# The input product of a fused RWKV-6 and GELU-MLP kernel: seven products of halves for tiles 2 to 7, and attention in finer, planned slots

## The chip, the cores and the metric

The kernel runs on one core of a Trainium2 chip. The metric is device time in microseconds; lower is better. The core has TensorE (matrix products, written to PSUM), VectorE, ScalarE and GpSimd (elementwise work), and queues that issue DMA transfers; SyncE and ScalarE issue the ones that matter here. Each engine takes its instructions in the order in which the program gives them, and waits where an operand isn't ready or a buffer isn't free.

## The reference

Two blocks follow each other. The first is RWKV-6 attention over 4 batches, 8 heads, 768 steps and 48 channels: a state per head decays by `w` at each step and takes up `k` times `v`. Its output, with the heads side by side, is the input of an MLP with an exact GELU, 384 to 2048 to 384, over 3072 tokens.

```python
for t in range(S):
    kt, vt, rt, wt = (k[:, :, t], v[:, :, t], r[:, :, t], w[:, :, t])
    cur = np.einsum('bhd,bhe->bhde', u[None] * kt, vt)
    y[:, :, t] = np.einsum('bhd,bhde->bhe', rt, state + cur)
    state = wt[:, :, :, None] * state + np.einsum('bhd,bhe->bhde', kt, vt)
...
h = x @ w_in
g = 0.5 * h * (1.0 + erf(h * inv_sqrt2))
return (g @ w_out).astype(np.float32)
```

## The kernel before

The 3072 tokens are cut into eight tiles of 384, two for each batch. For each tile there are two programs, both Python generators. `attention(x, unit)` (L318) issues the attention of tile x and leaves the output, transposed, in `xT`. `mlp(x)` (L782) turns `xT` into output rows. A loop at L1076 runs eight stages: in stage x it walks through `mlp(x - 1)` and, at the steps listed in `place`, lets `attention(x)` go on by one slot, that is up to its next `yield`; `place_next` does the same for the first slots of `attention(x + 1)`, and `times` for the pieces of the next tile's load. The order of the instructions on every engine follows from these lists alone. Tile 0 runs ahead of the loop with its own slots.

**Attention of tiles 2 to 7.** Time within a chunk of 64 steps is treated by quarters at two levels, `QUARTERS = (4, 16)`. First VectorE multiplies r, u and k (L356), makes running products of w (`tot`, L375), products for distances 1 to 3 within four steps (`apart`, L350) and their sums with a transposing reduction (L343), and folds w into r and k (L379). ScalarE (`plain`, L502) and VectorE (`lay_out`, L507 and L508) then lay out r for a level in `kx`. A burst of 96 small matmul records on 64x64 tiles of the array (L529, at the first level with L522 ahead of it) makes the blocks of a level in three pairs of PSUM banks, and VectorE copies them under a mask into `a_sb` (L560, L567). r and k are updated for the next level (L536, L542, L545). After the second level k is transposed in blocks (L481), moved by DMA (L476) and by ScalarE (L591), and three more bursts follow: k times v (L607) with the chain of states on VectorE (L622), blocks times v (L648), and r times states (L689). ScalarE copies the result to `xT` (L712); one quarter of the heads goes through `ysb` (L715) and six DMAs (L719).

**The MLP.** w_in (three chunks of 128 rows) and w_out stay in SBUF. For tiles 0 to 6 h is computed plainly: for each of 16 blocks of 128 columns three matmuls of 384 columns into one of two PSUM banks (L886), and GELU on ScalarE (L889, L891). The output product is done plainly for tile 0 (L1023), and for the others as seven products of halves, 192 columns wide (L900), with sums of g and of w_out made by VectorE; the last 128 rows of two tiles are combined likewise.

Only in the last tile is h itself made from seven products of halves (`h_halves`, L813, matmuls at L840), over the first two of the three chunks and both halves of tokens and columns; four products remain for the third chunk. Here VectorE adds the intermediate sums (L852 to L866), six PSUM banks are used, and attention is over. `h_sums` (L746) makes sums of w_in and differences of `xT` for it in the stage before. The third block of 128 rows of the last tile is a plain product (L929).

PSUM has eight banks: two, with the tag `mm`, serve h and the output products, and three pairs (`pd`, L91) serve attention.

Of the kernel before, what the change touches and what calls it, by code (L numbers as in the profile page):

```python
# [20 lines left out]
C = 64  # L21
# [15 lines left out]
HALFWAY = 2  # L37

# [6 lines left out]
def kernel(  # L45
# [45 lines left out]
    pd = pairs_of_banks.enter_context(tc.tile_pool(name="pd", bufs=3, space=PSUM))  # L91
# [29 lines left out]
    def load_v(x, dma):  # L121
        loaded[x][1] = io.tile([128, v.shape[2]], F32, name="v_in")
        dma.dma_start(out=loaded[x][1], in_=v[x])
# [10 lines left out]
    def load(x, dma):  # L134
# [4 lines left out]
        for i in range(3):  # L139
            if i == 1:  # L140
                load_v(x, dma)
                yield
            t = bufs[x % 2 if i == 0 else 1]
            for j in range(3):
                a = i * ALL + j * ALL // 3
                dma.dma_start(out=t[:, a:a + ALL // 3], in_=rkw[x, :, a:a + ALL // 3])
                yield

# [39 lines left out]
    def keep_warm(n, elsewhere=False):  # L188
        if elsewhere:
            t = pd.tile([128, 2, BANK], F32, name="warm", tag="d")[:, 0]  # L190
# [66 lines left out]
    def make_quarter_masks():  # L257
        make_fine()
        for (h, a), m_q in m_qs.items():
            nc.vector.tensor_tensor(out=quarter[h][a], in0=s_qs[h][:, 0:m_q.shape[1]], in1=m_q, op=ALU.is_equal)  # L260

# [3 lines left out]
    tot_sb = const.tile([128, NP * T], F32, name="tot_sb")  # L265

# [3 lines left out]
    def conversion():  # L270
# [5 lines left out]

        prepare(i + HALFWAY)
        if wide:
# [20 lines left out]
    def finish(dst, raw, f, e):  # L299
# [9 lines left out]
        nc.vector.tensor_scalar(out=f, in0=f, scalar1=3, scalar2=None, op0=ALU.logical_shift_left)  # L309
        nc.vector.scalar_tensor_tensor(out=e, in0=hi, scalar=0x80000000, in1=e,  # L310
# [7 lines left out]
    def attention(x, unit):  # L318
# [34 lines left out]
        if x >= 2:  # L353
            for q in range(qs):
# [3 lines left out]
                                               op0=ALU.mult, op1=ALU.mult)  # L358
            transposed_sums(0, 0, FINE)
# [11 lines left out]
        for h in LEVELS:  # L371
# [4 lines left out]
            at_tot += nb  # L376
        if x >= 2:
            def times(z, by):
                nc.vector.tensor_mul(z, z, by)  # L379

            places_of = [apart(1, 3)]
            times(k4[:, :, 0:2], w4[:, :, 1:3])
            places_of.append(apart(2, 2))
            times(k4[:, :, 0:1], w4[:, :, 2:3])
            places_of.append(apart(3, 1))
            yield
            for e, place in enumerate(places_of, 1):
                transposed_sums(place, e, FINE - e)

            w_01 = tot[2].rearrange("p (m two) -> p m two", two=2)[:, :, 0:1]  # L390
            times(k4[:, :, 0:3], w4[:, :, 3:4].to_broadcast([128, n_m, 3]))
            times(r4[:, :, 3:4], w4[:, :, 2:3])
# [6 lines left out]
        def products(bs, right, width):  # L399
            d = pd.tile([128, 2, BANK], F32, name="d", tag="d")  # L400
# [20 lines left out]
        def halves():  # L421

            for h in LEVELS:
# [9 lines left out]
                if h == 1:  # L433
                    yield
                    diag = diagonal()

# [13 lines left out]
                else:  # L450
                    nc.vector.tensor_mul(rk, rk, tt)  # L451
                ah = at.rearrange("p g n (m two j) -> p g n m two j", two=2, j=h)[:, :, :, :, 1, :]
# [16 lines left out]
        kt_q = w.rearrange("p (g n d) -> p g n d", g=2, d=G)  # L469
# [15 lines left out]
        def quarters():  # L485
# [26 lines left out]
            yield  # L512
            for h in QUARTERS:
                m, r4, t4, s0, s1, s2 = views(h)
                banks = [pd.tile([128, 2, BANK], F32, name="d", tag="d") for _ in range(0, np_ * NI, 4)]
                if h == FINE:

                    n_b = np_ * NI
                    fine_ps = [banks[-1][:, g, 6 * C:6 * C + FINE * n_b] for g in range(2)]
                    for a in range(FINE):  # L520
                        for g in range(2):
                            nc.tensor.matmul(fine_ps[g][:, a * n_b:], lhsT=places[half[g], a], rhs=fine_sb[half[g], 0:FINE - a, a],  # L522
                                             start=(a == 0), stop=True, skip_group_check=True)
                ds = []
                for n, d in zip(range(0, np_ * NI, 4), banks):
                    for i in range(4):
# [645 lines left out]
```

## Time and profile before

| | |
|---|---|
| runs | 604.7, 605.21 and 606.0 us, median 605.21 |
| span of the profiled execution | 601.5 us; the median of the runs is 3.7 us above it, and the page gives no other time of its own for this execution |
| TensorE busy | 589.7 us |
| VectorE busy | 468.3 us |
| ScalarE busy | 178.3 us |
| h of tiles 0 to 6 (L886) | 672 records, 223.0 us |
| output products of halves (L900) | 1120 records, in five groups |
| h of the last tile (L840) | 176 records, 28.60 us in the chain |
| masked copies of the quarter blocks (L560) | 108, 45.1 us |

PE stands for TensorE, PEld for its weight loads, DVE for VectorE, ACT for ScalarE, SP for SyncE; a q behind a name is the engine's queue. A line of the chain gives the start, the length, and the engine, tile, line and number of instructions of a piece. A line of the timeline gives the start and the length, the engine, the line, the operation, what it writes and reads, and in brackets how long the engine stood idle before it and what released it. One fp32 matmul is recorded as two instructions, and so is its weight load. The ends of matmuls are modelled, so starts are safer than ends.

### The profile page before, as it was taken

The page shows a single profiled execution, that of the slowest core. Times are in us where ns is not written, and L with a number is a line of the kernel's source. Part 1 is how long each engine was busy: PE and PEld are TensorE (multiplying, and loading weights), DVE is VectorE, ACT ScalarE, POOL GpSimd, SP SyncE. Part 2 cuts the span into 40 slices and gives each one's busy share as a digit, 9 for nine tenths or more (in the row PEclk, how much of TensorE's full clock was granted, in tenths as well). Part 3 has the DMA queues.
Part 4 walks back from the last instruction along what each step waited for, and adds up shares of the span by engine and source line. Part 5 has one row for each costly group of instructions (what it writes and reads, how often), then busy time and mean ns, then how long its engine had stood idle before and what let it go on. Part 6 is the DMA issues. An engine that isn't in the chain of part 4 may idle for free.

```text
span 601.5 us, 16134 instructions
## 1 busy us (share of the span) xinstructions
PE 589.7 (98%) x7008; PEld 455.8 (76%) x7008; DVE 468.3 (78%) x898; ACT 178.3 (30%) x414; POOL 8.4 (1%) x24
## 2 busy tenths in 40 slices
PE   8889999999999999999999999999999999999997
PEld 4566666656698669986699568995689668999977
DVE  7988999998876978488884987679786888665701
ACT  2355376123222322213222232113222133024400
POOL 3100000000000000000000000000000000000000
PEclk9999999999999999999999999999999999999999
DMA  5677348112142304303043303213042002010000
GB/s 198 209 218 260 107 159 303 35 34 76 17 99 77 92 2 93 90 21 93 1 95 90 99 1 65 90 51 92 3 94 90 8 1 40 16 38 8 1 14 26
DMA packets 50566, 46.72 MB, mean 78 GB/s; under 512 B 31680, under 2 KB 35904, under 8 KB 50496
## 3 DMA queue, kind: packets, MB, share of 16 engines
q1 hardware_dynamic: 33152, 29.31, 15.8%
q10 hardware_dynamic: 17344, 16.39, 9.9%
q8 instruction: 55, 0.90, 0.6%
q14 instruction: 15, 0.12, 0.1%
HBM read 36.24 MB, written 4.72 MB: 68 GB/s over the span
## 4 chain that ended last, share of the span: by engine, by line
PE 93%; DVE 5%; issue 1%; ACT 0%; DVEq 0%
PE h_ps L886 35%; PE o_ps L900 31%; PE o_ps L1023 5%; PE b L840 5%; PE d L529 4%; PE d L406 3%; PE kv_ps L607 2%; PE y_ps L689 2%; PE y_ps L648 2%; PE warm L194 2%; PE o_ps L929 2%; DVE rkw L451 1%; PE d L522 1%; DVE a_sb L461 1%; DVE a_sb L417 1%
## 5 line engine op out<-in xcount | busy, mean ns | idle before, releaser
L886 PE MATMUL h_ps<-xT,w_in_sb 128*128 128x384 f32 x672 | 223.0, 489 | 0.0
L886 PEld LDWEIGHTS h_ps<-xT,w_in_sb 128*128 128x128 f32 x672 | 125.9, 190 | 84.6 <-ACT xT L696 0.4
L889 ACT ACTIVATE g<-h_ps 128x384 f32<-128x384 f32 (+1 forms) x112 | 49.5, 444 | 169.4 <-PE h_ps L886 169.4
L900 PE MATMUL o_ps<-t,s 128*128 128x192 f32 x480 | 81.9, 329 | 0.0
L900 PEld LDWEIGHTS o_ps<-t,s 128*128 128x128 f32 x480 | 77.8, 190 | 0.7
L560 DVE COPY_PREDICATED a_sb<-quarter,d 128x384 f32<-128x384 uint8 (+2 forms) x108 | 45.1, 438 | 2.5
L900 PE MATMUL o_ps<-w_out_sb,g 128*128 128x192 f32 x224 | 38.7, 326 | 0.0
L900 PEld LDWEIGHTS o_ps<-w_out_sb,g 128*128 128x128 f32 x224 | 37.0, 190 | 1.9
L622 DVE SCALAR_TENSOR_TENSOR st<-st,tot_sb,kv_ps 128x48 f32<-128x48 f32 x160 | 29.0, 257 | 4.2 <-PE kv_ps L607 4.1
L1023 PE MATMUL o_ps<-w_out_sb,g 128*128 128x384 f32 x96 | 32.2, 491 | 0.0
L406 PEld LDWEIGHTS d<-rkw 64*64 64x64 f32 x1152 | 19.3, 138 | 13.3 <-DVE rkw L451 7.8
L900 PE MATMUL o_ps<-w_out_sb,s 128*128 128x192 f32 x160 | 28.3, 330 | 0.0
L900 PE MATMUL o_ps<-t,g 128*128 128x192 f32 x160 | 27.6, 326 | 0.0
L1023 PEld LDWEIGHTS o_ps<-w_out_sb,g 128*128 128x128 f32 x96 | 17.7, 190 | 12.3 <-DVE o_sb L1029 0.6
L343 DVE TRANSPOSE_TENSOR_REDUCE rkw<-kx 128x48 f32<-128x1536 f32 (+3 forms) x24 | 26.8, 1155 | 0.2
L529 PEld LDWEIGHTS d<-kx,rkw 64*64 64x64 f32 x1152 | 24.3, 133 | 3.4 <-DVE a_sb L567 1.6
L529 PE MATMUL d<-kx,rkw 64*64 64x96 f32 x1152 | 26.5, 245 | 0.0
L900 PEld LDWEIGHTS o_ps<-t,g 128*128 128x128 f32 x160 | 26.3, 190 | 0.0
L900 PEld LDWEIGHTS o_ps<-w_out_sb,s 128*128 128x128 f32 x160 | 25.9, 190 | 0.4
L406 PE MATMUL d<-rkw 64*64 64x64 f32 (+1 forms) x1152 | 21.7, 224 | 3.9 <-DVE rkw L451 2.3
L542 DVE TENSOR_TENSOR rkw<-rkw,tot_sb 128x768 f32<-128x768 f32 x12 | 11.5, 958 | 17.4 <-PE d L529 17.4
L379 DVE TENSOR_TENSOR rkw<-rkw 128x384 f32<-128x384 f32 (+2 forms) x24 | 23.6, 1006 | 0.4
(149 smaller groups left out, 744.0 us busy)
## 6 DMA issues: line engine op xcount, KB each, us to landing
rkw<-in_rkw_dram ACTq DMA_DIRECT2D x45, 256.0 KB, 2.8
raw<-in_w_out_dram SPq DMA_DIRECT2D x8, 768.0 KB, 4.3
out_dram<-o_sb SPq DMA_DIRECT2D x21, 192.0 KB, 1.9
raw<-in_w_in_dram SPq DMA_DIRECT2D x5, 768.0 KB, 7.6
v_in<-in_v_dram ACTq DMA_DIRECT2D x5, 584.0 KB, 3.6
raw<-in_w_in_dram SPq DMA_DIRECT2D x9, 256.0 KB, 3.9
rkw<-in_rkw_dram SPq DMA_DIRECT2D x8, 288.0 KB, 3.8
rkw<-in_rkw_dram SPq DMA_DIRECT2D x9, 256.0 KB, 7.2
```

The lines of the kernel that those rows point to most:

```text
L194: nc.tensor.matmul(t, lhsT=zeros[:, 0:128], rhs=zeros, start=True, stop=True)
L343: nc.vector.tensor_reduce(out=fine_sb[:, e, 0:n].rearrange("p a n -> p (a n)"), in_=kx[:, o:o + n * n_m].rearrange("p (m j) -> p m j", j=3 ...
L379: nc.vector.tensor_mul(z, z, by)
L406: nc.tensor.matmul(d[half[p], g, n * width:(n + 1) * width], lhsT=kc[half[g], b, i, p], rhs=right(half[g], b, i, p), start=True, stop=True)
L529: nc.tensor.matmul(d[half[p], g, i * 3 * C // 2:(i + 1) * 3 * C // 2], lhsT=kc[half[g], (n + i) // NI, (n + i) % NI, p], rhs=rx[half[g], 2 ...
L560: nc.vector.copy_predicated(out=an[:, :, :, :, (a + 1) * h:], mask=mask.to_broadcast(data.shape), data=data)
L622: nc.vector.scalar_tensor_tensor(out=stq[:, q, c], in0=stq[:, q, c - 1] if c else b4[:, q, NC - 1], scalar=totq[:, q, c:c + 1], in1=kvs[q ...
L840: nc.tensor.matmul(o, lhsT=lhsT, rhs=rhs, start=start and i == 0, stop=(i == len(factors) - 1), skip_group_check=True)
L886: nc.tensor.matmul(h_ps, lhsT=w_in_sb[:, f // FI, j, f % FI * 128:(f % FI + 1) * 128], rhs=xT[:, j, :], start=(j == 0), stop=(j == NJ - 1))
L889: nc.scalar.activation(out=gs[group][:, f % FG, 0:t], in_=h_ps[:, 0:t], func=AF.Gelu)
L900: nc.tensor.matmul(o, lhsT=lhs(j), rhs=rhs(j), start=start and j == 0, stop=(j == HF - 1), skip_group_check=True)
L1023: nc.tensor.matmul(o, lhsT=block(i, f // HF, f % HF), rhs=w_out_sb[:, f, :], start=(f == 0), stop=(f == NF - 1))
```

## The change

**h by halves from the third tile on.** In `mlp(x)` for x above 1, `h_halves` takes the place of the plain product. It is a generator now, with a `yield` after each product. It works on two blocks of columns at a time, which share a bank as two halves of 192. The seven products with their four companions are grouped as `first` to `seventh`. Intermediate sums aren't added by VectorE any more: ScalarE copies a partial sum to another PSUM bank or to g, TensorE accumulates onto the copy in PSUM, and only two adds per pair of blocks remain on VectorE (in `third` and `seventh`). GELU then works in place on two blocks at once.

**Sums.** `h_sums` makes the sums of w_in once, in stage 2, one of them in place in w_in; `first_sum` changes one quarter of w_out in place. `sums_of_x` makes five differences of halves of `xT` for each tile 2 to 7, one of them in place. `homes` finds room for them where the raw weights were.

**Banks.** After stage 1 `fewer_pairs` closes the three pairs and opens two pairs and two single banks (`bank_u`), which it sets with a matmul of zeros each.

**Attention in finer slots.** A burst of a level is cut into parts of 5, 5 and 2 chunk pairs, each in its own slot, with the masked copy of the first part between the second and third. At the level 16 the copies are done by ScalarE on blocks of partitions instead of by VectorE with a mask. Most of the other slots are cut too: 43 now for a tile.

**The plan.** The lists `place`, `place_next` and `times` are replaced by a string per stage in `PLAN`. A letter lets one generator go on by one step: `.` the MLP, `s` the tile's attention, `f` the next tile's, `l` the load, `x` the differences of `xT`, `w` masks and sums of weights, `c` weight conversion. The output products can be left after half of their matmuls.

**Others.** k transposed takes k's place instead of w's, the load of the next tile takes r, w, k and v in this order, v has one buffer, and the third row block of the last tile is made from four half products.

```diff
+    3: (
+        "..s..ls.ss..ss..ss.s....s.....s.ssl.l.ss..sss.s.sss..sl..lss..s.ssss.s.s......lss.sllssl.s"
+        ".f.slf..s.ff.x.x.xffffffxx"
+    ),
...
+    5: (
+        ".s.s.s.ss..s..sl.s..s..s....s.ll.sssss...sssss.l..s....sss.l.s.l.sss.ss.s..s..s..sl.sl.s.."
+        ".slfs.ffs..xlx.x.fffxx"
+    ),
...
+    def fewer_pairs():
+        pairs_of_banks.close()
+        pools["d"] = ctx.enter_context(tc.tile_pool(name="pe", bufs=2, space=PSUM))
+        pools["u"] = ctx.enter_context(tc.tile_pool(name="pu", bufs=1, space=PSUM))
+        for i in range(2):
+            u = bank_u(i)
+            nc.tensor.matmul(u, lhsT=zeros[:, 0:128], rhs=zeros, start=True, stop=True)
...
-        kt_q = w.rearrange("p (g n d) -> p g n d", g=2, d=G)
+        kt_q = k.rearrange("p (g n d) -> p g n d", g=2, d=G)
...
+                def copy_quarters(first, behind, d):
+                    d = d[:, :, 0:(behind - first) * 3 * C // 2].rearrange("p g (n x) -> p g n x", n=behind - first)
+                    if m == 1:
+
+                        for p in range(2):
+                            for a, rows in ((1, slice(0, 2 * h)), (0, slice(0, h)), (2, slice(2 * h, 3 * h))):
+                                z = slice(p * 64 + rows.start, p * 64 + rows.stop)
+                                o = (0, 3 * C // 4, 5 * C // 4)[a]
+                                nc.scalar.copy(out=at[z, :, first:behind, (a + 1) * h:],
+                                               in_=d[z, :, :, o:o + (3 - a) * h])
+                        return
...
+                cuts = (0, 5, 10, n_b)
+                parts_of = list(zip(cuts, cuts[1:]))
+                ds = [burst(*parts_of[0])]
+                yield
+                ds.append(burst(*parts_of[1]))
+                yield
+                copy_quarters(*parts_of[0], ds[0])
+                yield
+                ds.append(burst(*parts_of[2]))
+                yield
...
+    def sums_of_x(x):
+
+        xT = xT_of[x]
+        x00, x01, x10, x11, l0, l1 = (xT[:, c, b * HT:(b + 1) * HT] for c in range(3) for b in range(2))
+        t2, t3, t4, l01 = x_sums
+        for o, a, b in ((t3, x11, x01), (x01, x01, x00), (t2, x11, x01), (t4, x10, t2), (l01, l0, l1)):
+            nc.vector.tensor_sub(o, a, b)
+            yield
...
+            def two(o, q, *factors, start=False):
+                for i in range(2):
+                    for n, (lhs, rhs) in enumerate(factors):
+                        multiply(o[:, i * HT:(i + 1) * HT], lhs(2 * q + i), rhs, start and i == n == 0)
...
+            def saved(o):
+                z = wk.tile([128, DM], F32, name="o_sb", bufs=2)
+                nc.scalar.copy(out=z, in_=o)
+                return of_two(z)
+
+            def first(q):
+                a_of[q] = h_bank()
+                two(a_of[q], q, (w(0, 0), x00), start=True)
+                u_of[q] = bank_u(q)[:, 0:2 * HT]
+                nc.scalar.copy(out=u_of[q], in_=a_of[q])
+
+            def second(q):
+                two(a_of[q], q, (w(0, 1), x10), (w(0, 2), l0))
+                gelu(q, 0, 0, of_two(a_of[q]))
+                if q:
+                    gelu(q - 1, 0, 1, g_of(q - 1, 0, 1))
+
+            def third(q):
+                two(z_of[q], q, (s(4), x11), (w(0, 2), l1))
+                z = saved(z_of[q])
+                nc.vector.tensor_add(g_of(q, 0, 1), g_of(q, 0, 1), z)
+
+            def fourth(q):
+                two(u_of[q], q, (w(1, 1), t4), (w(1, 2), l01))
+                gelu(q, 1, 0, of_two(u_of[q]))
+
+            def fifth(q):
+                z_of[q] = h_bank()
+                two(z_of[q], q, (s(1), t1), start=True)
+                nc.scalar.copy(out=g_of(q, 1, 1), in_=of_two(z_of[q]))
+
+            def sixth(q):
+                two(u_of[q], q, (s(2), t2))
+                nc.scalar.copy(out=g_of(q, 0, 1), in_=of_two(u_of[q]))
+
+            def seventh(q):
+                two(u_of[q], q, (s(3), t3), (w(1, 2), l1))
+                z = saved(u_of[q])
+                nc.vector.tensor_add(g_of(q, 1, 1), g_of(q, 1, 1), z)
...
+            for q in range(HK):
+                first(q)
+                yield
+                if q:
+                    third(q - 1)
+                    yield
+                    seventh(q - 1)
+                    yield
+                else:
+                    fifth(q)
+                    yield
+                second(q)
+                yield
+                if q:
+                    fifth(q)
+                    yield
+                sixth(q)
+                yield
+                if q:
+                    fourth(q - 1)
+                    gelu(q - 1, 1, 1, g_of(q - 1, 1, 1))
+                    yield
```

## The prediction

> **What bounds the kernel now.** I read the page's head first, for who is busy.
>
> ```profile
> span 601.5 us, 16134 instructions
> PE 589.7 (98%) x7008; PEld 455.8 (76%) x7008; DVE 468.3 (78%) x898; ACT 178.3 (30%) x414; POOL 8.4 (1%) x24
> ...
> PEclk9999999999999999999999999999999999999999
> ```
>
> TensorE is busy for 98% at full clock. Busy is no proof, so I read the chain that ended last in order of time: one tile, then the last tile.
>
> ```profile
> 329.78 17.41 PE h_ps L886 x54
> 347.20 0.99 PE d L522 x16
> 348.19 2.14 PE d L529 x96
> 350.33 9.87 PE h_ps L886 x30
> 360.20 2.14 PE d L529 x96
> 362.35 4.07 PE h_ps L886 x12
> 366.41 7.80 PE o_ps L900 x48
> ...
> 541.01 28.60 PE b L840 x176
> 569.61 10.32 PE o_ps L929 x32
> ```
>
> From 71.9 us to 598 us the chain is TensorE alone, so the instruction stream of that engine is the time. Each fp32 matmul is two records. A 384-column record takes 17.41/54 = 0.3224 us, a 192-column one 28.60/176 = 0.1625 us. VectorE is second: it prepares the operands that the attention bursts (L522, L529) wait for. The timeline of the same tile shows how closely:
>
> ```profile
> 344.61 0.96 DVE L379 TENSOR_TENSOR rkw<-rkw,tot_sb 128x768 f32<-128x768 f32 x1
> ...
> 345.60 1.34 ACT L502 COPY kx<-rkw 128x384 f32<-128x384 f32 x3 [1.75 <-DVE rkw L379]
> ...
> 346.56 0.96 DVE L508 TENSOR_TENSOR kx<-kx,tot_sb 128x768 f32<-128x768 f32 x1 [0.40 <-ACT kx L502]
> ...
> 348.12 2.21 PE L529 MATMUL d<-kx,rkw 64*64 64x96 f32 x96
> ```
>
> L508 ends at 347.52 and the burst that reads kx starts at 348.12, with L522 run meanwhile: no slack is left over.
>
> **What the skill says.** "TensorE: Matmul & The Clock Gate", the table at its head: ScalarE and VectorE are strict FIFO. The trace agrees: L502 idles 1.75 us for VectorE, with nothing from behind it passing. "TensorEngine Tiling (Array Packing)", Key Properties: changing the tiling mode drains TensorE. The trace agrees in kind: two L689 bursts of 80 and 96 records (timeline, end of 64x64 work to the next 128x128 work) take 1.52 and 1.76 us from the expected end of the product ahead to the start of the next; the slope is 0.015 us a record, which leaves 1.76 - 96 x 0.015 = 0.32 us per burst that doesn't depend on its size.
>
> **The change, part by part.**
>
> A. h of tiles 2 to 6. Out go 96 records of 384 columns, 30.94 us a tile; in come 8 x 11 products, 176 records of 192, at the pace that the last tile's L840 already shows, 28.60. Saved 2.34 a tile, 11.7 in five. The last tile had this count before.
>
> B. The last tile's third row becomes 64 records of 192, 10.40 against L929's 10.32: +0.1.
>
> C. Two zero matmuls that set up the new banks: +0.5 (the warm ones take 0.23 each).
>
> D. Each quarter level's burst of 96 is cut into three. Reading the plan strings slot by slot, tiles 2 to 7 have 5, 6, 4, 4, 4, 6 separate sittings on TensorE for the two levels against 2 each before: 17 more. At 0.32 us: +5.4. The low bound is 0.13 (in the first tile, bursts of 48 between warm matmuls cost 0.934 and of 96 between h groups 1.733: 0.135 fixed if the neighbours cost alike), the high 0.43 (L529 takes 2.35 with its edges, 1.92 as pure streaming at 1.2 columns a ns on four tiles). The seven joints inside a sitting: +0.7.
>
> E. The stage of tile 1 loses about 2.3 us of TensorE idle now (L406 waits for L451, and 0.94 once); finer conversion slots may recover some: -0.7.
>
> A to E: -11.7 + 0.1 + 0.5 + 5.4 + 0.7 - 0.7 = -5.7. That is the floor if TensorE waits for nothing new: 599.5.
>
> F. Waits. ScalarE gets 20 copies of 384 more per fast tile (L502's 0.45 to 0.5 each: 9.6 us) and the 18 block copies of the level 16 (estimate from the skill's "ScalarE: Activation LUTs", What ACT_TABLE_LOAD costs, 186 ns + 0.833 ns an element: 0.32 to 0.59 each, 6 to 7 us). VectorE loses 9 of L560 (3.8) and gains 8 adds of 384 (L507's 0.55 each, 4.4) and 5 differences of 192 (0.3 each, 1.5). Neither fills up: VectorE works about 114 us in two tiles of 134. What matters is the order around a tile's end. Before, 48 records (7.8 us) lie between L689 and the next h; the plan leaves 4 half products, 5.2 us (3.9 for tile 2). The end of L689 to the finished xT:
>
> ```profile
> 387.00 2.57 PEld L900 LDWEIGHTS o_ps<-w_out_sb,s 128*128 128x128 f32 x16
> ...
> 387.14 0.48 ACT L715 COPY ysb<-y_ps 128x384 f32<-128x384 f32 x1 [5.62 <-PE y_ps L689]
> ...
> 387.65 1.21 ACTq L719 DMA_DIRECT2D xT<-ysb  x2
> ...
> 389.87 1.93 ACT L712 COPY xT<-y_ps 48x384 f32<-48x384 f32 x4
> ```
>
> xT is whole 4.8 us after L689 ends (call that end zero). Take the stage of tile 5. The five differences wait for xT, so they are done at 6.3. Behind them VectorE runs, by this trace's spacings: the rest of the totals 1.2, L350 with L379 2.2 + 2.6 + 1.7, three L343 2.6, L379 3.8, lay-out 1.9 (together 16.0), and ahead of the lay-out three new adds, 1.6: ready at 23.9. TensorE starts h at 5.2 and has 100 records up to the first burst, 16.25 us: it arrives at 21.5 and waits 2.4 us. The same walk for the others, with the slots where each plan puts them. Tile 3: h starts at 4.8 with xT, the burst is due 18.2 later at 23.0; the differences end at 8.1 (the totals lie between), plus 16.0 and four adds of 2.0 is 26.1: 3.1 late. Tile 4: the L350 and L343 groups (9.1) stand ahead of the last two differences, which end at 15.8, and the fourth product of the first pair needs them at 14.3: 1.5. Tile 6: the last two end at 12.7, then 1.7 + 2.6 + 3.8 + 1.9 and adds of 1.6 make 24.3, the burst is due at 20.8: about 3.4. Tile 7: 10.1, then 12.6 and 1.6 make 24.3 against 21.5: 2.8. The sum is 13; overlapping starts and early operands can shorten each by some tenths, so I take 2.0 a stage, +10. Tile 2 runs on plain h and waits for nothing new. What is queued behind: gelu of the third block waits on ScalarE for a VectorE add in the same queue, so fifth and sixth copies come late too; that lies inside the same delay, not on top. Once late, TensorE can't recover it, as nothing else in the stage bounds it.
>
> Bounds of F: 0 (if the lay-out is ready in time) to 15 (the walk, and 2 for ScalarE). Moved DMAs: k's pieces now follow the state products on ScalarE's queue and v's load the y burst, because v has one buffer; each blocks the queue only until a burst that TensorE has just issued, and the next tile's first use lies some 4 us later against 2.8 us landing. I cost that at nothing; if a piece lands late, VectorE starts a stage up to 1 us later and F grows by as much.
>
> The sum is -5.7 + 10 = +4.3 on a span of 601.5: 605.8. The median of the runs is 3.7 above the span (605.2), so 609.5. About 0.2%, or 1.2 us, is what a measurement tells from no change.
>
> **The rivals.**
>
> R1, the plan is in time, and the time falls to the floor. For it: before, the burst also came 0.6 us after its operand with no loss on the chain, so slots can be put exactly; and the L840 pace held in the last tile with VectorE and ScalarE working beside it. Against it: the walk. It decides when the lateness is under 5.7/5 = 1.1 us a stage. 599.5, and 596 with the low price of D.
>
> R2, ScalarE bounds the products. A pair of f takes 44 records, 7.15 us, in which ScalarE has 9 operations of 0.48, 4.3 us; with no attention every copy is done about 1.9 us before its reader. A burst of six block copies (2.2 to 2.7) or of ysb, its DMAs and the xT copies (4.7) exceeds that. At 0.5 us four times in each of six stages: +12 on the floor, 611.5. Against it: most of these bursts lie in the products' half of the tile, where ScalarE has one copy in 2.6 us.
>
> R3, only the two pairs of banks bind: the third burst of a level needs the first one's pair copied out. In tiles 4 and 6 one burst (0.85) and one half product (1.3) lie between, against 2.2 to 2.7 of ScalarE's copies; about 0.5 a stage, +2.5 to 3: 602 to 602.5. Against it as the whole: it presumes that VectorE is in time at the first burst.
>
> **How the numbers follow.** The late lay-out 0.47, R1 0.26, R2 0.13, R3 0.14. The likeliest has its own range 605.5 to 615 (lateness 1.2 to 3.1 a stage). Slower: 0.42 of the first, 0.12 of R2: 0.54. Within 0.2%: 0.05 of the first, 0.02 of R3, 0.04 between the cases: 0.11, of which the last comes off R1. Faster: 0.22 of R1 and 0.12 of R3, and 0.01 of R2: 0.35. The range that leaves out 2 in 10 runs from 597.5 (most of R1) to 615.
>
> **What would show it.** A: h records at 0.1625 us with 0.32 gone, 28.6 us a tile as their sum. D: nine attention sittings in tiles 3 and 7. F: in the waits, weight loads of the first L529 burst of a tile idle 1 to 3 us for VectorE's lay-out (or ScalarE's plain copies), in each of tiles 3 to 7, and TensorE's share falling to about 96%. R1 would show none of these; R2 waits of the fifth to seventh products on ScalarE's copies throughout; R3 idle only ahead of third bursts. The prediction is wrong if xT is whole sooner after L689 than 4.8, or if VectorE gets through the stretch from the differences to the lay-out in under 16 us.

## The result, and the profile after

The changed kernel takes 621.54 us (median of four runs, 618.53 to 622.88) against 604.96 for the kernel before (four runs, 602.64 to 606.0): a ratio of 1.028, with a 95% interval of 1.0246 to 1.0315. It is slower, by 16.6 us; the forecast was 609.5, and its range ended at 615. The profiled execution has a span of 619.1 us, 17.6 above the span before.

The head of the changed kernel's page:

```profile
span 619.1 us, 17176 instructions
PE 593.4 (96%) x7442; PEld 514.2 (83%) x7442; DVE 460.7 (74%) x878; ACT 262.3 (42%) x604; POOL 8.4 (1%) x24
...
PEclk9999999999999999999999999989999999999999
```

ScalarE works 84 us more, VectorE 8 us less, and neither is near full. TensorE's share fell by two points, and one slice of its clock row shows an 8 where the row before had none.

The chain of work that ended last, in the same stage as the one shown of before, tile 5 (start, length, what):

```profile
350.22 3.66 DVE rkw L435 x4
353.90 1.00 ACT kx L568 x3
...
356.01 1.05 PE d L596 x40
357.07 1.50 PE u_ps L925 x8
...
404.74 1.60 PE y_ps L791 x96
406.37 0.49 ACT ysb L817
...
409.19 4.23 DMA xT<-ysb
413.50 0.37 DVE s L893
```

Before, this chain was TensorE alone. Now VectorE, ScalarE, a queue and a transfer are in it, at two places of the stage: ahead of the first burst, and at the tile's end between the last y burst (L791) and the first product of the next h. The waits of TensorE say the same (total us, times, longest):

```profile
PE o_ps L1065 <- ACT o_sb L1122: 2.4, 2, 1.8
...
PE h_ps L925 <- DMA xT<-ysb: 2.0, 1, 2.0
PE d L596 <- ACT g L957: 1.8, 2, 1.2
PE h_ps L925 <- ACT rkw L1159: 1.6, 2, 1.3
PE h_ps L925 <- ACT g L988: 1.6, 2, 1.2
```

No wait is large. They are many, of one or two us, and most name ScalarE.

**Where 17.6 us come from.** I measured TensorE from start to start of its records, with the paces of the prediction (0.1625 us for a record of 192 columns, 0.322 for 384), from the first h product of tile 0 on. The first such product comes 1.3 us later than before; the stage of tile 1, from there to the first h product of tile 1, is 3.7 us shorter (79.9 for 83.6); the stages of tiles 2 to 7 and the last half stage are together 20.0 us longer (495.1 for 475.1). In these:

| part | us |
|---|---|
| records of h and output products (A and B) | -11.5 |
| 17 more sittings at 0.355 us, measured below (D) | +6.0 |
| h of the next tile waits at its start, and ten records at half pace | +8.6 |
| output products wait for ScalarE's copies of o_sb | +5.1 |
| products of h wait for GELU, copies and differences | +4.7 |
| bursts of the two levels wait for the lay-out or a pair of banks | +3.2 |
| the k times v burst waits for ScalarE's blocks of k | +1.6 |
| gaps too small to name | about +2 |

The saving is there in full. In a long stage, one of an odd-numbered tile, h and the output products had 96 records of 384 columns and 192 of 192, which is 62.14 us at these paces; now they have 368 of 192, which is 59.80, 2.34 less as forecast. It is paid for twice over by waits, some 25 us.

Three places show how such a wait comes about. First, stage 2, in the output products:

```profile
168.75 2.71 ACTq L542 DMA_DIRECT2D rkw<-kx  x4
...
171.50 2.60 ACT L612 COPY a_sb<-d 32x320 f32<-32x320 f32 x6 [3.66 <-DMA rkw<-kx]
...
174.12 0.32 ACT L1122 COPY o_sb<-o_ps 128x192 f32<-128x192 f32 x1
...
174.50 1.73 PE L1065 MATMUL o_ps<-w_out_sb,f 128*128 128x192 f32 x9 [1.81 <-ACT o_sb L1122]
```

ScalarE first issues four transfers (2.7 us), then makes six block copies of the level 16 (2.6 us), and only then copies the finished output product out of its bank. That copy takes 0.32 us, but it stands last, and TensorE needs the bank. Second, the end of tile 5:

```profile
406.88 2.90 SPq L821 DMA_DIRECT2D xT<-ysb  x4
...
408.38 0.96 ACT L814 COPY xT<-y_ps 48x384 f32<-48x384 f32 x2 [1.53 <-issue]
408.88 0.33 ACTq L170 DMA_DIRECT2D v_in<-in_v_dram  x1
409.35 1.93 ACT L814 COPY xT<-y_ps 48x384 f32<-48x384 f32 x4
...
413.50 0.36 DVE L893 TENSOR_TENSOR s<-xT 128x192 f32<-128x192 f32 x1 [3.29 <-DMA xT<-ysb]
413.67 4.59 PE L925 MATMUL h_ps<-xT,w_in_sb 128*128 128x192 f32 x16 [1.97 <-DMA xT<-ysb]
```

The copies into xT end at 411.3, but the transfers from ysb only at 413.4: at 408.88, 0.31 us ahead of the issue of the sixth and last of them (409.19, by the chain above), the load of the next v (584 KB) has been issued. The sixth lands 4.23 us after its issue. TensorE stands 2.13 us, and its next ten records run at 0.32 us instead of 0.1625.

The third place is the one that the prediction named, the first burst of a tile. The list of waits puts it down to a GELU (L957). The timeline of tile 5 tells otherwise:

```profile
354.91 0.96 DVE L574 TENSOR_TENSOR kx<-kx,tot_sb 128x768 f32<-128x768 f32 x1
...
355.51 0.49 ACT L957 ACTIVATE g<-h_ps 128x384 f32<-128x384 f32 x1
...
356.01 0.43 PE L596 MATMUL d<-kx,rkw 64*64 64x96 f32 x9 [1.17 <-ACT g L957]
```

The burst reads nothing of g. It reads kx, whose last part L574 ends at 355.87, and starts 0.14 us after that. The GELU happened to end at 356.00, just after it, and that is why the list names it.

### The profile page after: what moved, and what is told of

Its sections match the earlier page's. It is cut to its first block, busy times and chain, and to the rows that moved or that the text cites. A ratio compares the mean times of both kernels' runs of the same rounds, so it can differ in the third digit from the quotient of the medians.

```text
span 619.1 us, 17176 instructions
## 1 busy us (share of the span) xinstructions
PE 593.4 (96%) x7442; PEld 514.2 (83%) x7442; DVE 460.7 (74%) x878; ACT 262.3 (42%) x604; POOL 8.4 (1%) x24
## 4 chain that ended last, share of the span: by engine, by line
PE 40%; DVE 16%; ACT 6%; ACTq 2%; DMA 2%; issue 2%; SPq 1%; DVEq 0%
PE o_ps L1065 15%; PE u_ps L925 8%; PE h_ps L925 8%; DVE kx L401 3%; DVE rkw L435 3%; PE d L596 3%; ACT a_sb L612 2%; DVE rkw L394 2%; PE u_ps L1065 2%; ACTq L542 1%; ACT xT L814 1%; PE kv_ps L706 1%; DMA xT<-ysb 1%; PE y_ps L747 1%; SPq L821 1%
## 5 line engine op out<-in xcount | busy, mean ns | idle before, releaser
L925 PE MATMUL h_ps<-xT,w_in_sb 128*128 128x192 f32 x480 | 97.3, 335 | 6.2 <-DMA xT<-ysb 2.0
L1051 PE MATMUL h_ps<-xT,w_in_sb 128*128 128x384 f32 x192 | 64.2, 490 | 0.1
L612 ACT COPY a_sb<-d 32x320 f32<-32x320 f32 (+5 forms) x108 | 39.2, 363 | 23.8 <-DMA rkw<-kx 11.2
L925 PE MATMUL u_ps<-s,w_in_sb 128*128 128x192 f32 x192 | 35.9, 330 | 0.8 <-DVE s L893 0.8
L925 PEld LDWEIGHTS u_ps<-s,w_in_sb 128*128 128x128 f32 x192 | 31.4, 190 | 1.9 <-issue 1.0
L1065 PE MATMUL o_ps<-w_out_sb,f 128*128 128x192 f32 x160 | 28.5, 329 | 2.4 <-ACT o_sb L1122 2.4
L1065 PE MATMUL o_ps<-w_out_sb,e 128*128 128x192 f32 x160 | 28.4, 329 | 1.1 <-ACT o_sb L1128 1.1
L1054 ACT ACTIVATE g<-h_ps 128x384 f32<-128x384 f32 (+1 forms) x32 | 13.9, 435 | 36.1 <-PE h_ps L1051 35.9
L1065 PEld LDWEIGHTS o_ps<-w_out_sb,f 128*128 128x128 f32 x160 | 26.1, 190 | 3.2 <-ACT o_sb L1122 3.0
L1065 PE MATMUL o_ps<-t,s 128*128 128x192 f32 x160 | 28.4, 330 | 0.0
```

Source lines behind the costliest of these rows:

```text
L612: nc.scalar.copy(out=at[z, :, first:behind, (a + 1) * h:], in_=d[z, :, :, o:o + (3 - a) * h])
L925: nc.tensor.matmul(o, lhsT=lhsT, rhs=rhs, start=start, stop=True, skip_group_check=True)
L1051: nc.tensor.matmul(h_ps, lhsT=w_in_sb[:, f // FI, j, f % FI * 128:(f % FI + 1) * 128], rhs=xT[:, j, :], start=(j == 0), stop=(j == NJ - 1))
L1054: nc.scalar.activation(out=gs[group][:, f % FG, 0:t], in_=h_ps[:, 0:t], func=AF.Gelu)
L1065: nc.tensor.matmul(o, lhsT=lhs(j), rhs=rhs(j), start=start and j == 0, stop=(j == HF - 1), skip_group_check=True)
```

## The experiments

Theory 1 was that xT comes late at the tile's end; theory 2, that ScalarE's queue holds TensorE's banks; the prediction's own theory, that VectorE's lay-out is late ahead of the first burst and that everything else follows from that. Line numbers in each experiment are those of its own kernel. Medians come from different chips, so I compare the ratio to the kernel before, measured beside each, and the spans. The spans have a disturbance of their own: the first h product of tile 0 came between 42.9 and 45.5 us in ten kernels with the changed program (42.8 in two traces of the old one), though none of the edits lies ahead of it. So I also give the later part, by which I mean the time from the first h product of tile 1 to the end, where all the edits lie: 475.1 us before and 495.1 in the changed kernel. It comes from a single trace of each kernel.

### h reads other data than xT

```diff
-        xT = xT_of[x]
+        xT = w_out_sb[:, HF:HF + NJ, :]
...
-        for o, a, b in ((t3, x11, x01), (x01, x01, x00), (t2, x11, x01), (t4, x10, t2), (l01, l0, l1)):
+        for o, a, b in ((t3, x11, x01), (t1_home, x01, x00), (t2, x11, t1_home), (t4, x10, t2), (l01, l0, l1)):
```

These lines are from `sums_of_x`; `h_halves` reads the same three blocks and the same `t1_home`.

> The changed kernel, but the h products of tiles 2 to 7 and the five differences read three blocks of w_out (and a constant tile) in place of xT, so nothing of h waits for the y burst, its copies or the ysb transfers; the instructions are the same in number and size (h is then not that of the reference). Theory 1, xT late at the tile's end: the waits of the first h products (6.9 us in six stages, and 1.6 us of half clock behind the longest) go: 7 to 9 us less than the changed kernel, 612.5 to 614.5. Rival, the late lay-out of my prediction: TensorE only arrives earlier at the first burst of a tile and waits there instead, 0 to 3 us less.

Measured: ratio 1.0207 (1.0176 to 1.0238), a span of 614.0, 5.1 less than the changed kernel. That lies between the two expectations. But 1.2 of it lies in the earlier start of the first h product; the later part is 4.1 shorter. The waits of TensorE show what was left:

```profile
PE h_ps L926 <- ACT rkw L1161: 2.9, 3, 2.3
...
PE d L597 <- ACT o_sb L963: 1.7, 2, 0.8
```

Of 8.6 us at the start of h, 3.4 stayed, and they don't need xT: L1161 copies an output product (`p1_alone`) out of its bank, and stands in ScalarE's queue behind the ysb copy, two DMA issues and six copies into xT. In stage 2 the wait even grew, from 1.47 to 2.46. At the first burst of tile 6 it grew by 0.2, of tile 5 it shrank by 0.3: the rival, that the gain is taken back there, isn't seen. What was taken back stands elsewhere: 0.7 us more at an output product in the stage of tile 7, and a new 0.7 in the last y burst of tile 6. Theory 1 holds for 5.2 us of waits, of which 4 come out in the time; the 3.4 that stayed belong to theory 2.

### The level 16 copied by VectorE again

```diff
-                    if m == 1:
+                    if False:
```

> The changed kernel, but the level of 16 is copied by VectorE through masks as before, so ScalarE loses 108 block copies (39 us in all) and VectorE gets its nine masked copies a tile back (3.8 us a tile). Theory 2, ScalarE's queue: the waits of output products for o_sb copies and of the k v burst behind block copies go, 3 to 6 us less, 615.5 to 618.5. Rival, VectorE is what comes late (the prediction): its later work moves 3.8 us further back in each tile and 2 to 8 us are added. If ScalarE's queue only sees copies wait that nobody waits for: within 1 us.

Measured: ratio 1.0245 (1.0206 to 1.0283), a span of 615.2, 3.9 less; the later part is 4.2 shorter. By ratio alone this can't be told from the changed kernel (1.0246 to 1.0315); the list of waits is clear. The waits of output products for o_sb (L1122, L1128) are gone; the 0.61 of the last tile, which is for another copy, stays. New ones stand in the list:

```profile
PE d L596 <- DVE a_sb L621: 2.9, 2, 1.4
...
PE kv_ps L706 <- DVE a_sb L621: 1.3, 1, 1.3
```

They are third bursts of the level 16 in tiles 4 and 6 (1.5 us each), which wait for the first pair to be copied out, now by VectorE, and the k times v burst of tile 3. So theory 2 is right on what held the output products. The block copies moved VectorE's load to where TensorE waits for ScalarE; moving it back makes it wait a little for VectorE. The rival, that 3.8 us more on VectorE per tile come out as 2 to 8 us more, is refuted.

### Both

> The edits of e1_other_xT and e2_masked together (h of tiles 2 to 7 reads other data than xT, so it is not that of the reference; the level of 16 is copied by VectorE through masks). Alone they took 5.1 and 3.9 us off the span of the changed kernel (619.1). If the two causes are separate: 9.0 less, a span of 610.1. If both only show one chain that comes late (VectorE's order of work behind it takes over): 5 to 6 less, 613 to 614. What is left then over the span of the kernel before (601.5) is the price of the sittings and the waits for ScalarE's and VectorE's work inside h.

Measured: ratio 1.0161 (1.012 to 1.0201), a span of 610.8, 8.3 less where 9.0 would be the sum; the later part is 7.7 shorter, where 8.3 would be. So the two causes are separate, or nearly. They explain 8 of some 25 us of waits. No experiment takes the waits inside h (4.7) or those of the first bursts (2.2) by itself.

### The price of a sitting

The kernel before, with nothing changed but one cut in each level's burst. The cut fell after 32 of the 96 records, not after 48 as the expectation says.

```diff
                 for n, d in zip(range(0, np_ * NI, 4), banks):
+                    if n == 4:
+                        yield
                     for i in range(4):
...
-        place = [1, 3, 5, 7, 9, 11, 13, 15, 18, 20, 26, 32] if x == 1 else [1, 6, 8, 13, 15, 16, 18, 18, 20, 21]
+        place = [1, 3, 5, 7, 9, 11, 13, 15, 18, 20, 26, 32] if x == 1 else [1, 6, 8, 9, 13, 14, 15, 16, 18, 18, 20, 21]
```

> The kernel before, with each quarter level's burst of 96 cut once, in two sittings of 48 with h or output products between: 12 more sittings in six tiles, and nothing else changed. By the trace of the changed kernel (three sittings of a level cost 0.71 us more than one) 0.355 us each: 4.3 us more than before, 609.3. By the prediction's 0.32: 3.8. By its low bound of 0.13: 1.6. If a cut sitting costs waits too, more than 6.

Measured: ratio 1.0204 (1.0174 to 1.0234), a span of 614.0, 12.5 above before. TensorE's timeline in tile 7:

```profile
497.07 1.06 PE L522 MATMUL d<-rkw 64*128 64x48 f32 x16
498.06 0.89 PE L531 MATMUL d<-kx,rkw 64*64 64x96 f32 x32
498.88 2.20 PE L888 MATMUL h_ps<-xT,w_in_sb 128*128 128x384 f32 x6
501.01 1.55 PE L531 MATMUL d<-kx,rkw 64*64 64x96 f32 x64
```

From the end of one h product to the start of the next, the two sittings take 1.91 and 1.57 us, and 0.10 goes lost behind each; the one sitting of before took 3.23 and 0.10. So a cut costs 0.35 us, the same at the second level (0.91 and 1.57 for 2.23). The stage of tile 7 is longer by just two of these, 0.71. Twelve cuts are 4.3 us. The other 8.1 are what the last line of the expectation allowed for, waits. Most are of one kind:

```profile
PE kv_ps L609 <- DMA rkw<-kx: 5.1, 5, 1.5
```

VectorE's work behind a burst waits for the later half, the blocks of k come that much later, their transfers too, and the burst of k times v stands 1.2 to 1.9 us in five of six tiles (7.0), an output product 1.05 once. This is the whole case in small: here the cuts cost TensorE 4.3 us, and their delay cost 8 further on, where nothing else in the order was moved with them.

### h of tiles 2 to 6 multiplied plainly

```diff
-        if fast:
-            yield from h_halves()
+        if fast and not final:
+            yield from h_plain()
+        elif fast:
+            yield from h_halves()
```

`h_plain`, which the edit adds, is not shown.

> The changed kernel with h of tiles 2 to 6 as plain products (96 records of 384 columns, one gelu a block, no half products, spread over the same 25 slots; their weights and xT are those of the halves, so h is not that of the reference). Part A of the prediction: the stream of TensorE gets 11.7 us longer. If the waits are not made by the half products: 11 to 12 us more than the changed kernel, 633. If the chain of copies between the half products costs what the waits on gelu and copies inside h show (3.8 us): 7 to 9 us more. If the half products bring all of the new waits: 0 or less.

Measured: ratio 1.1009 (1.095 to 1.1068), a span of 662.7. None of the three expectations, and the edit is at fault: `sums_of_x` writes one difference over a half of xT, so a plain product that reads all of xT must wait for VectorE's difference, and the output products, left in their order, wait too (7.1 us at one line).

```profile
PE h_ps L1053 <- DVE xT L893: 15.2, 5, 4.0
```

On the half products it tells nothing. It tells something on the clock: the mean granted clock was 0.977, and behind each of its six idle stretches of 3.24 us or more TensorE ran 4 to 16 records at half pace.

### The load of v at the end of tile 5

```diff
-        ".slfs.ffs..xlx.x.fffxx"
+        ".slfsl.ffs..xx.x.fffxx"
```

> The changed kernel with one letter of the plan string of tile 5 moved: the load of the next v (584 KB) is issued behind the first y burst and ahead of the last, in place of just behind the ysb transfers that make xT whole. In the changed kernel xT came 4.2 us after the issue of those transfers there, TensorE stood 2.13 us and ran its next ten records at half pace (1.6 us). If the v load that runs beside them is the cause: that wait and the half pace go, 3 to 4 us less than the changed kernel, 617.5 to 618.5, and xT is whole about 2 us earlier. If those transfers are late for another reason: nothing changes at that place.

Measured: ratio 1.0281 (1.0255 to 1.0307), no change; a span of 618.4, 0.7 less. At the place the expectation is met:

```profile
403.93 0.33 ACTq L170 DMA_DIRECT2D v_in<-in_v_dram  x1
...
406.98 0.48 ACT L817 COPY ysb<-y_ps 128x384 f32<-128x384 f32 x1 [1.27 <-PE y_ps L791]
...
412.18 0.36 DVE L893 TENSOR_TENSOR s<-xT 128x192 f32<-128x192 f32 x1 [1.36 <-DMA xT<-ysb]
412.35 0.89 PE L925 MATMUL h_ps<-xT,w_in_sb 128*128 128x192 f32 x4
```

The transfers from ysb are now done 5.2 us behind the copy L817's start instead of 7.1, TensorE waits 0.20 instead of 2.13, and all its records have full pace. The load of v beside them was the cause. But right behind, an output bank (L1188) is waited for 0.57 us instead of 0.30, a GELU 0.79, the first burst 0.2 more, and the next tile's h 0.5 more: half of the 3.6 gained at the place is taken by what was late next. And the stage ahead, which the edit doesn't touch, began with 1.25 us of wait where the changed kernel had 0.57. The later part is 0.9 shorter in all.

### Other plan strings

The changed kernel's work, with the letters `.` of tiles 2 to 7 at other places between the attention slots, one `f` and one `x` exchanged in tile 3, and the parts of the level 16 copied by VectorE in tiles 3, 4 and 7 and one each in 2 and 6. So two things change together, the order and the engine of some copies. Of tile 5, and the choice of the engine (`PAR` has a letter for each part, `a` for ScalarE):

```diff
-        ".s.s.s.ss..s..sl.s..s..s....s.ll.sssss...sssss.l..s....sss.l.s.l.sss.ss.s..s..s..sl.sl.s.."
-        ".slfs.ffs..xlx.x.fffxx"
+        "...s.s.ss.s...s.sl.s.s..s....sll.sssss....sssss.l.s....ss.sl.slss.s..sss...s...s..slsl.s.sl"
+        "f.s.ff.s..xlx.x.fffxx"
...
-                    if m == 1:
+                    if m == 1 and PAR[x][0][parts_of.index((first, behind))] == "a":
```

> The changed kernel with other plan strings for tiles 2 to 7 (the half products and product halves stand at other places between the same attention slots, in the same order; fewer separate sittings), the level of 16 copied by VectorE through masks in tiles 3, 4 and 7 and in parts of 2 and 6, by ScalarE elsewhere. No work is added or taken away. If the waits come from where the plan puts the slots, and not from the seven products or the two pairs of banks as such: 12 to 17 us less than the changed kernel, 605 to 610. If they come with the halves or the banks whatever the order: within 3 us of the changed kernel.

Measured: 608.3 us, ratio 1.0057 (1.0039 to 1.0076), a span of 607.9, 11.2 less than the changed kernel, and 2.2% less by the ratios; the median lies within the 605 to 610 that were expected if the order is the cause. The later part is 12.2 shorter. Nine sittings are saved (23 for the two levels in all tiles against 29, and in three tiles the two y bursts in one), which is 3.2 us; the other 9 are waits. So most of the loss is neither in the seven products nor in the two pairs of banks as such, for both are still there. It is in where the plan put their slots and in which engine copies the level 16. These two weren't taken apart: by the experiment with all of the level 16 on VectorE, up to 4 of the 9 can be the engine's. The largest wait left is that for the ysb transfers of tile 5 again: 2.46 us, and nine records at half pace.

Two edits on top of it, each alone:

```diff
-        "f.s.ff.s..xlx.x.fffxx"
+        "f.sl.ff.s..xx.x.fffxx"
```

> v1_plan with the one letter of e7_v_earlier moved: in tile 5 the v load is issued between the two y bursts. In v1_plan TensorE stood 2.46 us there for xT and ran at half pace after it (1.7 us). In the changed kernel the same move freed 3.6 us at the place and only 0.7 us of the span, as what follows (the lay-out for the first burst, copies inside h) was itself late. If v1_plan has slack there, the span falls by 3 to 4 (607.9 to about 604); if the next wait takes it, by 1 or less.

Measured: ratio 1.0023 (1.0007 to 1.0039), 2.1 us less than the other plan by the ratios; at the place TensorE waits 1.00 us at full pace, and the two stages concerned are 2.45 us shorter. Here more of the gain stays. The expected 3 to 4 was too high: 1.00 us is now waited for ScalarE's copies into xT, and 0.74 at a GELU behind.

```diff
-        if x == 1:
+        if x == 2:
             fewer_pairs()
```

> v1_plan with the three pairs of banks kept until stage 2 is issued (the call of fewer_pairs at x == 2 in place of x == 1); nothing else is changed. Tile 2 then has a third pair for the third part of each level. In v1_plan the first level of tile 2 took 4.44 us in one sitting of 112 records (3.39 by the spacing of its parts), about 1.0 of it a wait for the first pair. Expected: 1.0 to 1.5 less, a span of 606.5 to 607. If the bank isn't what it waits for: nothing.

Measured: ratio 1.0054 (1.0035 to 1.0073), no difference in time that could be told. In the trace the sitting of tile 2 takes 3.39 us instead of 4.44, as expected, and the stage is 0.7 shorter; 0.1% is below what these runs resolve. The later part is 2.7 shorter in this trace, and most of that has nothing to do with the edit: at the end of tile 5, where v is loaded as in the other plan, TensorE waited 1.58 us here and kept full pace, against 2.46 and half pace there. So one place varies by more than 2 us from trace to trace, and of the last two experiments the ratios say more than the traces.

### A version under both kernels

The other plan with both edits (the v load moved in every tile where it stood beside the ysb transfers), its strings adjusted once more, and an order in the last tile in which one output product stands between a copy and the product that needs it:

```diff
                 nc.scalar.copy(out=right, in_=left)
+                yield from product(o2, of_blocks(1, 1), of_t(3), True)
                 yield from product(left, of_blocks(2, 1), of_w(1, 0))
```

> As v1_plan, and three more edits: in no tile does the v load run beside the ysb transfers, the third pair of banks is given up one tile later (tile 2 still multiplies h plainly and needs no bank for the halves), and in the last tile one output product stands between the copy of a bank and the product that overwrites it (0.61 us of wait). By the waits seen in v1_plan: the stage that starts with the wait of 2.46 us and the half pace loses 4, tile 2 loses 1.5, the last 0.6, so 6 less than v1_plan: 602 to 603, some 0.3% under the kernel before. If the waits only move on: within 2 us of v1_plan, 606 to 610.

Measured: 603.71 us (15 runs) against 604.6 (19 runs), ratio 0.9982 (0.9972 to 0.9992): 0.18% faster than the kernel before, a little short of the 0.3% expected, and 2.9% faster than the changed one. Its page:

```profile
span 601.0 us, 17129 instructions
...
PE 583.7 (97%) x7426; PEld 512.5 (85%) x7442; DVE 474.5 (79%) x911; ACT 238.2 (40%) x538; POOL 8.4 (1%) x24
```

From the first h product to the end it takes 556.4 us, against 558.7 before and 575.0 in the changed kernel; its first h product comes 1.9 us later than before. But where the seven products are, it gains nothing on the kernel before: the stage of tile 1 is 4.4 us shorter, and the later part takes 477.2 us against 475.1. About 10 us of waits remain there, and nine sittings more than before (3.2 us); together they eat more than the 11.7 of h. What makes this version's trace shorter is the stage of tile 1, part E of the prediction.

## Why the prediction was wrong

**A, B and C were right.** h lost 2.34 us a tile at the pace that the last tile had shown, the last tile's third row cost about 0.2, and the two zero matmuls took 0.43.

**D was right within about a tenth.** 0.355 us for a sitting where 0.32 was taken, 6.0 for 17 instead of 5.4. The low bound of 0.13 is excluded. "TensorEngine Tiling (Array Packing)" of the Trainium skill, Key Properties, says that a change of the tiling drains the array, and gives no price; in these kernels a sitting more, with its change there and back, costs 0.355 us.

**E was too careful.** The stage of tile 1 got 3.7 us shorter, not 0.7, though the first h product came 1.3 later. What moved that start isn't settled: it varied by 2.6 us among kernels that are alike there. With that the floor came out at about -8 where the text had -5.7, so the whole miss lies in the waits.

**F failed, as the term of the sum and as a mechanism.** It put 10 us of waits (bounds 0 to 15) at one place, the first burst of tiles 3 to 7; the waits came to some 25. That mechanism exists: the lay-out ended 0.14 us ahead of the burst in tile 5, and TensorE stood 1.23 and 0.71 us in tiles 5 and 6. But in tiles 3, 4 and 7 it stood for nothing there, so it is 1.9 us in place of 10. The other waits, some 23, stand at places that the sum had at nothing. One duration behind that is the time of the transfers from ysb to xT, from issue to landing (the first line is for the end of tile 5 before, the second for the whole changed kernel):

```profile
DMA to landing us min/median/max: 1.9/2.0/2.8
...
DMA to landing us min/median/max: 1.8/2.1/4.2
```

The single steps of F:

- "xT is whole 4.8 us after L689 ends": that is where the six copies end. The last of the six transfers from ysb lands later, already in the stage of before that the walk took it from: 5.6 us after the burst. It took 2.8 us from its issue. Before, 48 records covered it. In the changed kernel xT is whole 5.0 to 7.1 us after the burst. Where TensorE already came late at h, the burst behind it had the more time, and the lateness that the walk expected later was taken earlier, at a place that it had not priced.
- "I cost that at nothing", of the moved DMAs: the load of v, now behind the y burst, slowed the transfers that make xT whole by 2 us, and cost 2.13 of wait and about 1.6 of half pace at one tile. The text asked when the load lands, not what is issued just behind it. The stages of before had the sign: in tiles 2 to 6 the sixth transfer is issued behind a load of 256 KB and takes 2.8 to 3.4 us, in tiles 1 and 7 there is no such load and it takes 1.9.
- "Tile 2 runs on plain h and waits for nothing new": 1.97 at an output product, 1.47 at the end, 0.26 at the burst.
- R2 was set at 0.13 with the argument that ScalarE's bursts "lie in the products' half of the tile, where ScalarE has one copy in 2.6 us". It is that one copy that counts. The skill's page "TensorE: Matmul & The Clock Gate" was cited for strict order on ScalarE, and the trace before agreed; but the walk followed only VectorE's order. Behind 2.7 us of DMA issues and 2.6 of block copies a copy of 0.32 us held a bank of the output products (one wait of 1.97; 5.1 us for all such waits), and behind the copies into xT another held a bank of h (3.4). With the waits for the blocks of k (1.6) and at the third bursts (0.8) that is some 11 us, close to the 12 that R2 put on top of the floor.
- The lines shown for the first burst of before have 0.6 us between the end of L508 and the burst, as R1 says; "no slack is left over" is too strong.

R1, the floor, was wrong as a forecast of this plan, and nothing that was run went below it: with other strings, fewer sittings, some copies back on VectorE and a few small edits the same work took 603.7 where R1 had 599.5. R3 was seen only as a part: 0.8 us in the changed kernel at third bursts, 3.0 where VectorE copies the level 16.

The direction was right, on thin ground: slower with 0.54. As most of the waits came where the walk had none, there is luck in that. The size was missed because the sum of waits was walked along one engine, and because one of its durations, the 4.8 us, was read too short.

## What to carry to other kernels

When a change removes cover at a place (here 48 records between the y burst and the next h became 4 half products), walk every queue through that place, not only the engine with the longest chain: here a copy of 0.32 us stood behind 5.3 us of issues and copies, and TensorE missed its bank for 1.97. A transfer that is needed within 5 us should not be issued just behind a large load. And a change that is right in its arithmetic can lose to its plan: the same products with other slots and some copies on another engine gave back 12 of 20 us, and the last version 18. So a slow result speaks against the plan first. The idea isn't cleared by that: even in the last version the tiles with seven products took 2.1 us longer than before, so whether they can pay here stays open.

## What the runs showed of the hardware

TensorE's half pace behind short waits was not expected. The first two lines are from the changed kernel, the other three from the run in which h reads other data than xT (window, length, then each engine's busy time and instructions, the granted clock, the share and the GB/s of the DMA engines):

```profile
410.35:413.76 3.41, 1.45 (x10) 1.18 (x9) 0.26 (x1) 0.92 (x2) 0.00 (x0) 1.00 0.62 221
413.76:417.17 3.41, 3.41 (x11) 3.13 (x12) 3.24 (x9) 0.94 (x2) 0.00 (x0) 0.50 0.31 82
...
189.51:192.92 3.41, 2.29 (x15) 2.00 (x13) 1.58 (x3) 2.07 (x5) 0.00 (x0) 1.00 0.24 54
192.92:196.33 3.41, 2.23 (x13) 2.04 (x14) 2.18 (x5) 2.03 (x5) 0.00 (x0) 1.00 0.52 193
196.33:199.74 3.41, 3.41 (x21) 3.19 (x21) 3.31 (x7) 1.43 (x3) 0.00 (x0) 1.00 0.21 55
```

In the clock record of every trace the stretches at half clock last 3.41 us or twice that (but for the last, which the end cuts off), and within a trace their starts lie whole multiples of 3.41 us apart. So I cut each trace into such windows, from 60 us to the last product, and counted, for those at full clock, from starts and paces how long TensorE stood in each. All eight windows with 2.4 us or more were followed by half clock, two of the five with 2.13 to 2.4, and none with less. What counts is the sum in one window, not the length of a wait. The wait of 2.13 us at 413.67 lies whole in one window; the one of 2.46 us at 194.10 in the other run is longer, but lies across a border, 1.28 and 1.18 us, and costs no clock. In the run with plain h a window with no wait above 1.04 us, but 2.47 in sum, was followed by half clock. "TensorE: Matmul & The Clock Gate", Part 1, says that the clock is halved after at least one idle window of about 3.4 us, with windows that run freely. The grid agrees with it; but a window needn't be idle throughout, so a wait of little more than 2 us can already cost another 1.7, half of a window.

ScalarE's queue issued the load of v (408.88) while four of the six copies that stand ahead of it in the program had not started; the last of them started at 410.81. So a DMA issue got ahead of queued copies on its own engine by 1.9 us, and ahead of the last ysb transfer too, which stands before it in the program but is the fourth of SyncE's queue. So the rule that each engine takes its instructions in the order of the program held here among ScalarE's copies and within each DMA queue, but not between them. Behind such a load the last transfer (24 KB) took 4.1 to 4.3 us in three traces, against 1.9 at the end of tile 2 of the changed kernel, where all six were issued ahead of the load.
